# Window attention with sink keys and a gated MLP on one core: batch 1's q and k as four long-run loads, score tiles by keys, and a new order of all steps

## The chip, the core and the metric

The kernel runs on one core of a Trainium2 chip. A core has five engines that run their own instruction streams: PE (TensorE: matmuls and transposes into PSUM), DVE (VectorE), ACT (ScalarE), POOL (GpSimd) and SP (SyncE, here only an issuer of DMAs). They meet through semaphores. PSUM has eight banks of 128 x 512 float32. The metric is the device time of one execution in microseconds (us), measured over several runs.

## What is computed

Inputs are q, k, v of 4 batches, 8 heads, 768 positions and 64 features in float32. A position attends to the 128 positions up to and with itself, and to the first 4 positions ("sink" keys). The attention's output x (768 x 512 a batch) goes through a gated MLP with spatial mixing:

```python
scores = scale * np.matmul(q, k.transpose(0, 1, 3, 2))
keep = (pos[None, :] < n_sink) | ((rel >= 0) & (rel < window))     # n_sink 4, window 128
a = softmax(np.where(keep, scores, -1e9))
x = np.matmul(a, v)                         # to (batch, 768, 512)
h = gelu_tanh(x @ w_in)                     # 512 -> 1024
u, v = h[..., :512], h[..., 512:]
v_n = (v - mean) / sqrt(var + 1e-6) * g_ln  # over the 512 features
v_s = np.einsum('ts,bsd->btd', w_sg, v_n) + b_sg[None, :, None]   # w_sg 768 x 768
out = x + (u * v_s) @ w_out                 # 512 -> 512
```

## The kernel before

Matmuls are in bf16, their sums in float32. All work is cut into small steps. A string, STEPS, lists them in one order, and each step emits its instructions in that order on its engine; there is no scheduler. The framework adds the semaphore waits that the data need. A step's numbers are its batch and its tile; a last letter names the engine (A for ACT, D for DVE, P for POOL). The work of neighbouring batches is interleaved by hand in this list, so that PE has scores of one batch beside the MLP of another.

A batch goes through these steps. q, k and v are loaded. Batch 0's q and k come in float32 by head pair from SP (LPQ, LPK, L243), in runs of 1536 bytes, each partition holding six consecutive positions, and are cast to bf16 (CPQ, CPK). The others' q and k come through POOL's DMA queue, which converts to bf16 (LQ, LK, L223): six loads each of 128 positions x 8 heads, in rows of 256 bytes, 128 KB written a load. LVH (L269) loads v by four heads. q and k are then turned so that the features are on the partitions: TQ and TK on PE (batch 0 by head pair, L371; batches 1 and 2 by two tiles, L377) with EQ and EK to bring them to SBUF (L197 on ACT, L198 on DVE); batch 3 by DMA transposes on SP (DQ, DK). The constant HOW = "GBBC" chooses this by batch.

QK (L478) computes transposed scores of a head pair and a tile of 256 queries: 256 matmuls of 128 or 256 columns, in three pieces per tile (two for the first). EX (L483, ACT) takes the exponential, MK masks it (DVE L490, POOL L493 and L496; a few tiles get the mask as a bias matmul, L473). KS, SK (L457) and SX (L462) do the same for the sink keys. AV (L519, L523, L526) multiplies with v, with a 65th column of ones that sums the weights; NR (L535, L536, DVE) divides by that sum, 36 steps of one head pair and two or three tiles. x is turned by XT and XE (L545), or by DMA (XD) for later batches.

The MLP: MV (L561) multiplies x with the second half of w_in, GV (L565, ACT) is its gelu, BN (L574 to L578, DVE) its mean and variance, RS (L583) the power -1/2, on POOL, NM (L586) and Z (L592 on ACT, L595 on DVE) normalise. MU (L602) and GU (L607) do the first half, u. WT (L614) and WE turn w_sg once. SP (L622, a step on PE that has its name by chance in common with the engine SP) is the spatial mix, GT (L627, DVE) applies g_ln and b_sg, GM (L632, DVE or POOL) multiplies with u. OU (L639) is the last product, RA (L643, DVE) adds x, and ST stores 256 KB from SP.

The weights' loads are issued by POOL too: LW (L275, two halves of w_in), LWS (L280, two halves of w_sg), LWO (L283, w_out), LB (L299, b_sg to all partitions). So POOL has masks, products, the powers RS and the loads in one stream. Steps WARM, FILL, MASK, IDEN and HM (matmuls on zeros at the start, L188) prepare.

Buffers come from rings that are used round robin. PSUM has two double banks for wide tiles (sc) and four single banks (mm). A step that takes a buffer waits until the last reader of its old content is done:

```python
sc_ring = Ring("sc", 2, [128, 2, 512], F32, psum)
mm_ring = Ring("mm", 4, [128, 512], F32, psum)
q16 = Ring("q16", 2, [128, NT * d_model], BF16)
```

Of the kernel before, what the change touches and what calls it, by code (L numbers as in the profile page):

```python
# [14 lines left out]
HOW = "GBBC"  # L15
VHOW = "HHHH"
# [4 lines left out]
WARM LPQ.0 FILL LPK.0 LPK.1 LPQ.1 LPQ.2 LG MASK LPK.2 LPK.3 CPQ.0.A VSK LPQ.3 IDEN CPK.0.A IDEN2 MASK0 HM.9 TQ.0.0  # L21
TK.0.0 EQ.0.0.D EK.0.0.A VSO HM.3 QK.0.0.0 ZERO CPK.1.P QK.0.0.1.1 EX.0.0.0 LVH.0.0 EX.0.0.1 QK.0.0.2.1 CPQ.1.D TK.0.1
EX.0.0.2 LC CPQ.2.D LVH.0.1 TQ.0.1 MK.0.0.0.D EK.0.1.A TQ.0.2 EQ.0.1.D EQ.0.2.A HM.2 QK.0.1.0 CPK.2.A CPK.3.P
QK.0.1.1.1 EX.0.1.0 LQ.1.0 CPQ.3.D TK.0.2 EX.0.1.1 TK.0.3 EK.0.2.D LQ.1.1 TQ.0.3 EK.0.3.A GTR EQ.0.3.D LW.0 QK.0.2.0
QK.0.2.1 EX.0.2.0 LK.1.0 KS.0 VSM.0 HM.2 SK.0.2 EX.0.2.1 SK.0.1 MK.0.2.0.D HM.4 AV.0.0.0 LW.1 QK.0.3.0.1 MK.0.1.0.D
SX.0.1 SX.0.2 QK.0.3.1 MK.0.2.1.P GCP.D NR.0.0.0 EX.0.3.0 AV.0.0.1 AV.0.1.0 AV.0.1.1 NR.0.0.1 EX.0.3.1 QK.0.1.2
NR.0.1.0 AV.0.2.0 AV.0.3.0 EX.0.1.2 MK.0.3.1.P NR.0.1.1 QK.0.2.2 AV.0.2.1 NR.0.2.0 EX.0.2.2 TQ.1.0 NR.0.3.0 MK.0.1.2.P
QK.0.3.2 AV.0.3.1 EQ.1.0.A NR.0.2.1 XT.0.0 NR.0.3.1 LWS.0 AV.0.0.2 EX.0.3.2 AV.0.1.2 XE.0.0.D LK.1.1 XT.0.1 MK.0.2.2.D
# [47 lines left out]
def kernel(  # L76
# [29 lines left out]
    NH = S // 2  # L106

# [3 lines left out]

    class Ring:
        def __init__(self, name, n, shape, dtype, pool=sb):
            self.tiles = [pool.tile(shape, dtype, name=f"{name}{i}") for i in range(n)]
            self.used = 0
            self.held = {}

        def new(self, key):
            t = self.tiles[self.used % len(self.tiles)]
            self.used += 1  # L120
            self.held[key] = t
            return t
# [7 lines left out]
    sc_ring = Ring("sc", 2, [128, 2, 512], F32, psum)  # L130
    mm_ring = Ring("mm", 4, [128, 512], F32, psum)
    q16 = Ring("q16", 2, [128, NT * d_model], BF16)
    k16 = Ring("k16", 2, [128, NT * d_model], BF16)
    qT = Ring("qT", 2, [128, NT * d_model], BF16)
    kT = Ring("kT", 2, [128, NT * d_model], BF16)
    P = Ring("P", 10, [128, 2, 512], BF16)
    exs = Ring("exs", 2, [128, 512], BF16)
    x_sb = Ring("x_sb", 2, [128, NT, d_model], BF16)
    xT = Ring("xT", 2, [128, NT, KD, 128], BF16)
    z = Ring("z", 2, [128, NT, d_half], BF16)  # L140
    uT = Ring("uT", 2, [128, KU, S], BF16)
    vt = Ring("vt", 3, [128, 2, d_half], F32)
    gtmp = Ring("gtmp", 4, [128, NH], BF16)
    ot = Ring("ot", 6, [128, d_model], F32)
    mvs = Ring("mvs", 2, [128, NT, 2], F32)
    rs = Ring("rs", 2, [128, NT], F32)
    nmr = Ring("nmr", 2, [128, NT], F32)
    v_sb = Ring("v_sb", 2, [128, H, NT, Dh + 1], BF16)
    v_sink = Ring("v_sink", 2, [128, H, Dh + 1], BF16)
    ks_w = 128 // HP  # L150
    ks_sink = Ring("ks_sink", 2, [128, HP, ks_w], BF16)

    c16 = Ring("c16", 6, [128, d_model], BF16)
    iden = sb.tile([128, 128], BF16, name="iden")
# [22 lines left out]
    def gated(b, hf):  # L177
        return gatedT[:, slots.setdefault((b, hf), len(slots) % 3)]
# [532 lines left out]
```

## Time and profile before

| what | value |
|---|---|
| time, median of 3 runs | 156.51 us (156.33 to 158.79) |
| the profiled execution's own time | 157.69 us |
| its span, first to last instruction | 156.0 us, TensorE clock granted 1.000 |
| DVE / ACT / POOL, share of the span | 79% / 64% / 64% |
| SP's DMA queue (hardware): packets, MB | 21544, 13.41 |
| PE busy, 0 to 10 / 10 to 20 / 20 to 30 us | 8.55 / 8.69 / 9.56 us |
| PE busy, 30 to 50 / 50 to 60 / 60 to 70 us | 20.00 / 8.85 / 9.30 us |
| PE busy, 70 to 150 us | 79.95 of 80 us |

How to read it: the profile is of one execution, so sums over its rows are set against that execution's span, not against the median. A matmul's end is modelled in the records, and matmuls are pipelined, so PE's busy share is an upper bound of the time in which it is at its rate; starts of successive instructions tell the rate. The chain that ended last is followed back from the last instruction to what released each one. In the timelines a row holds the start (us), the duration, the engine, the line, the operation, output <- inputs, the tile's shape, how many instructions were put together, and in brackets the idle time before them with what ended it. For a DMA issue the duration is that of the instruction that issues it; the transfer itself lands later.

### The profile page before, as it was taken

To read this page: it belongs to the slowest core of one execution; us is meant where nothing else is said; L and a number is where in the kernel's file an instruction comes from. 1 tells how busy PE (TensorE), PEld (TensorE's weight loads), DVE (VectorE), ACT (ScalarE), POOL (GpSimd) and SP (SyncE) were. 2 spreads that over 40 slices of the span, in tenths; PEclk is the share of its full clock that TensorE was granted. 3 is DMA by queue.
4 is the path that set the end of the run, shared out by engine and by line. 5 is a ranking of instruction groups with operands and counts; after the bars stand their busy time and mean duration, and the time that the engine had idled before them with its cause. 6 is when DMAs were issued, how large, how long until landed. Compare 5 with 4: busy or idle time off the path is not lost.

```text
span 156.0 us, 3856 instructions
## 1 busy us (share of the span) xinstructions
PE 146.7 (94%) x1549; PEld 94.2 (60%) x1549; DVE 123.4 (79%) x295; ACT 99.0 (64%) x110; POOL 99.3 (64%) x127
## 2 busy tenths in 40 slices
PE   6988989999999979989999999999999999999990
PEld 2445577779675756747566764486567644776530
DVE  4557789829989969969789887899789956867981
ACT  3699798799899846276897855269954025591000
POOL 4099779388999899997549869640798610300400
PEclk9999999999999999999999999999999999999999
DMA  4999999999999999999999199995710580510064
GB/s 156 282 365 151 153 197 189 166 192 193 146 143 142 193 152 139 167 156 156 168 230 246 22 285 174 178 197 60 236 71 3 102 235 0 202 63 11 0 227 179
DMA packets 86170, 24.67 MB, mean 158 GB/s; under 512 B 78660, under 2 KB 83016, under 8 KB 86152
## 3 DMA queue, kind: packets, MB, share of 16 engines
q0 software_dynamic: 64608, 11.01, 94.9%
q1 hardware_dynamic: 21544, 13.41, 33.1%
q8 instruction: 12, 0.20, 0.5%
q14 instruction: 6, 0.05, 0.1%
HBM read 24.81 MB, written 6.29 MB: 199 GB/s over the span
## 4 chain that ended last, share of the span: by engine, by line
PE 73%; DMA 17%; DVE 2%; POOL 2%; issue 1%; ACT 1%; SPq 1%; ACTq 0%
PE mm L622 17%; PE mm L639 14%; PE sc L561 13%; PE sc L602 12%; DMA w_out_sb<-in_moe_w_out_dram 7%; DMA v_sb<-in_v_dram 6%; PE sc L478 4%; DMA uT<-in_k_dram 4%; PE mm L519 3%; PE mm L377 3%; PE mm L523 2%; PE mm L526 2%; PE mm L614 1%; POOL v_sb L269 1%; PE mm L545 1%
## 5 line engine op out<-in xcount | busy, mean ns | idle before, releaser
L483 ACT ACTIVATE P<-sc 128x1024 bf16<-128x1024 f32 (+1 forms) x48 | 43.4, 953 | 10.3 <-PE sc L478 10.1
L622 PE MATMUL mm<-wsgT,z 128*128 128x384 bf16 x192 | 34.1, 327 | 0.0
L622 PEld LDWEIGHTS <-z 128*128 128x128 bf16 x192 | 17.7, 98 | 11.9 <-issue 0.7
L639 PE MATMUL mm<-w_out_sb,wsg_gated 128*128 128x512 bf16 x96 | 22.7, 379 | 1.1 <-DMA w_out_sb<-in_moe_w_out_dram 1.1
L561 PE MATMUL sc<-w_in_sb,xT 128*128 128x512 bf16 x96 | 22.2, 379 | 0.7 <-ACT vt L565 0.7
L627 DVE SCALAR_TENSOR_TENSOR gtmp<-mm,g_sb,b_bc 128x384 bf16<-128x384 f32 x32 | 19.1, 611 | 4.2 <-PE mm L622 3.6
L602 PE MATMUL sc<-xT,w_in_sb 128*128 128x256 bf16 x192 | 22.1, 273 | 0.0
L493 POOL TENSOR_SCALAR_AFFINE_SELECT P<-P 128x512 bf16<-128x512 bf16 x21 | 14.0, 667 | 12.3 <-ACT P L483 12.0
L632 POOL TENSOR_TENSOR wsg_gated<-gtmp,uT 128x384 bf16<-128x384 bf16 x15 | 14.5, 982 | 10.9 <-DVE gtmp L627 10.9
L574 DVE BATCH_NORM_STATS2 st<-vt 128x6 f32<-128x512 f32 x24 | 15.4, 685 | 7.5 <-ACT vt L565 7.4
L602 PEld LDWEIGHTS <-w_in_sb 128*128 128x128 bf16 x192 | 18.7, 98 | 3.0
L536 DVE TENSOR_TENSOR x_sb<-mm,rcp 128x384 bf16<-128x384 f32 (+1 forms) x36 | 18.5, 513 | 1.2
L643 DVE TENSOR_TENSOR ot<-mm,x_sb 128x512 f32<-128x512 f32 x24 | 16.1, 684 | 2.7 <-PE mm L639 2.5
L565 ACT ACTIVATE vt<-sc 128x1024 f32<-128x1024 f32 x12 | 12.3, 1027 | 9.0 <-PE sc L561 8.9
L583 POOL TENSOR_TENSOR rs<-rs,neg_half 128x4 f32<-128x4 f32 (+1 forms) x8 | 6.9, 867 | 17.4 <-DVE rs L578 16.0
L223 POOL DMA_DIRECT2D k<-in_k_dram x18 | 16.4, 928 | 0.7 <-DMA v_sb<-in_v_dram 0.7
L223 POOL DMA_DIRECT2D q<-in_q_dram x18 | 16.7, 952 | 0.0
L519 PE MATMUL mm<-v_sb,P 128*128 128x65 bf16 x192 | 15.9, 194 | 0.7 <-DMA v_sb<-in_v_dram 0.6
L519 PEld LDWEIGHTS <-P 128*128 128x128 bf16 x192 | 14.5, 98 | 2.8 <-issue 0.6
L639 PEld LDWEIGHTS <-wsg_gated 128*128 128x128 bf16 x96 | 9.2, 98 | 11.4 <-DMA w_out_sb<-in_moe_w_out_dram 1.4
L561 PEld LDWEIGHTS <-xT 128*128 128x128 bf16 x96 | 9.2, 98 | 10.9 <-issue 0.9
L478 PE MATMUL sc<-qT,kT 64*128 64x128 bf16 (+1 forms) x256 | 14.8, 238 | 0.6 <-DVE qT L198 0.3
(90 smaller groups left out, 244.4 us busy)
## 6 DMA issues: line engine op xcount, KB each, us to landing
out_dram<-ot SPq DMA_DIRECT2D x24, 256.0 KB, 2.3
v_sb<-in_v_dram POOLq DMA_DIRECT2D x8, 384.0 KB, 8.3
q<-in_q_dram POOLq DMA_DIRECT2D x18, 128.0 KB, 6.7
k<-in_k_dram POOLq DMA_DIRECT2D x18, 128.0 KB, 6.9
wsg_gated<-in_moe_w_sg_dram POOLq DMA_DIRECT2D x2, 576.0 KB, 8.3
w_in_sb<-in_moe_w_in_dram POOLq DMA_DIRECT2D x2, 512.0 KB, 10.2
uT<-in_q_dram SPq DMA_DIRECT2D x2, 384.0 KB, 3.2
uT<-in_k_dram SPq DMA_DIRECT2D x2, 384.0 KB
```

The costliest lines, as they stand in the source:

```text
L223: return nc.gpsimd.dma_start(out=dst.rearrange("p (h d) -> p h d", h=H), in_=heads(src, b, i))
L478: nc.tensor.matmul(sc[:, hl, c:c + 128 * ni], at(kT, b)[rows, j, p, :], at(qT, b)[rows, i:i + ni, p, :], start=not biased, stop=(not biase ...
L483: nc.scalar.activation(out=P.new((b, p, g))[:, :, 0:w], in_=sc_ring[b, p, g][:, :, 0:w], func=AF.Exp, scale=scale)
L519: nc.tensor.matmul(av[:, il, hl, :], pt[:, hl, c:c + 128], vb[:, h, i, :], start=first, stop=False)
L536: nc.vector.tensor_mul(x_sb.get(b)[:, i0:i0 + n, 128 * p:128 * (p + 1)].rearrange("p t (h d) -> p t h d", h=2), av[:, :, :, 0:Dh], rcp[:, ...
L561: nc.tensor.matmul(hp[:, jl, :], xT[b][:, 2 * g + jl, c, :], w_in_sb[:, c, d_half:2 * d_half], start=(c == 0), stop=(c == KD - 1))
L574: nc.vector.bn_stats(out=sts[jl], in_=vt[b, g][:, jl, :])
L602: nc.tensor.matmul(hp[:, dc // 2, 256 * (dc % 2):256 * (dc % 2 + 1)], w_in_sb[:, c, 128 * dc:128 * (dc + 1)], xT[b][:, 2 * g:2 * g + 2, c, :],
L622: nc.tensor.matmul(ps[:, 0:NH], z[b][:, si, 128 * dc:128 * (dc + 1)], wsgT[:, si, NH * hf:NH * (hf + 1)], start=(si == 0), stop=(si == NT ...
L627: nc.vector.scalar_tensor_tensor(out=gtmp.new((b, hf, dc)), in0=mm_ring["g", b, hf, dc][:, 0:NH], scalar=g_sb[:, dc:dc + 1], in1=b_bc[:, N ...
L639: nc.tensor.matmul(ps, gated(b, hf)[:, dc, 128 * tl:128 * (tl + 1)], w_out_sb[:, dc, :], start=(dc == 0), stop=(dc == KU - 1))
L643: nc.vector.tensor_add(ot.new((b, t)), mm_ring["o", b, t], x_sb[b][:, t, :])
```

## The change

1. **Loads.** Batch 1's q and k are loaded with two loads each of four heads. A partition holds six consecutive positions, so a run is 6 x 64 float32 = 1536 bytes; 384 KB are written a load. They take the place of twelve tile loads. They are turned by head pair: 8 TQ and TK with 12 transposes each in the place of 6 with 8, and the copy to SBUF puts the positions in order again (a stride of six). Batches 2 and 3 keep tile loads.
2. **Score tiles by keys.** Tile g holds the products of keys of tiles 2g and 2g+1 with all the queries that need them. There are two pieces of up to 256 columns per tile (192 matmuls in all). Tile g = 2, not 0, is the one of 384 columns.
3. **AV and NR by four heads.** A step has a tile of two PSUM banks. There are 18 of each instead of 36.
4. **PSUM and rings.** All of PSUM is one tile of eight banks. Which buffer a step gets is written out in a table, SLOTS, for all rings. gtmp has 3 buffers, not 4; the two v tiles were used in turn by the batches (0, 1, 0, 1) and now go 0, 0, 1, 1. The last batch's output rows are held in the q16 and k16 tiles.
5. **Order.** STEPS is written anew for all engines. There are 12 warming matmuls instead of 20; SK and SX of batch 0 are one step each instead of two; Z has 13 steps on ACT and 11 on DVE (9 and 15 before), MK 27 on DVE and 17 on POOL (23 and 21), GM 18 on DVE and 14 on POOL (17 and 15).

The core of the diff (the long new list is cut to the stretch around the first spatial mix):

```diff
-HOW = "GBBC"
-VHOW = "HHHH"
+LAYOUT = "SGBM"
...
-MV.0.0 XE.0.1.A LK.1.2 NR.0.0.2 MK.0.3.2.D LK.1.3 NR.0.1.2 AV.0.2.2 AV.0.3.2 LQ.1.2 NR.0.2.2 GV.0.0 MV.0.1 NR.0.3.2
-LQ.1.3 BN.0.0 LWS.1 XT.0.2 GV.0.1 MU.0.1 XE.0.2.A BN.0.1 WT.0 GU.0.1 TK.1.0 MV.0.2 RS.0.1 EK.1.0.A LK.1.4 NM.0.1
-WE.0.A WT.1 GV.0.2 LK.1.5 TK.1.1 MU.0.2 LB.P EK.1.1.A BN.0.2 Z.0.0.A LK.2.0 WT.2 GU.0.2 MU.0.0 WE.1.D RS.0.2 WE.2.D
-Z.0.1.A LQ.2.0 NM.0.2 Z.0.2.A Z.0.3.D Z.0.4.D WT.3 LQ.2.1 WT.4 GU.0.0 WE.3.D WT.5 LQ.1.4 Z.0.5.D TQ.1.1 QK.1.0.0
-EQ.1.1.D QK.1.1.0 LQ.1.5 SP.0.0.0 WE.4.D LK.2.1 EX.1.0.0 VSM.1 SP.0.0.1 WE.5.D EX.1.1.0 LVH.1.0 GT.0.0.0 TK.1.2 KS.1
...
+LPK.3 TQ.0.1 EQ.0.1.D CPK.3.D CPQ.2.A TQ.0.2 LVH.0.0 EX.0.0.2 LVH.0.1 LQ.1.0 TK.0.2 LK.1.0 EX.0.0.1 EK.0.2.A LK.1.1
+GTR LW.0 QK.0.1.2 QK.0.1.0 LWS.1 EX.0.1.0 LPQ.3 LC EX.0.1.2 TK.0.3 EQ.0.2.D QK.0.2.0 EX.0.2.0 CPQ.3.D TQ.0.3 EQ.0.3.A
+LW.1 VSM.1 EK.0.3.D MK.0.2.0.D MK.0.1.0.D QK.0.1.1.1 EX.0.1.1 KS.0 GCP.D QK.0.3.2 EX.0.3.2 QK.0.3.0.1 VSM.0 LK.2.4
+MK.0.1.2.P LWS.0 SK.0 MK.0.3.2.D AV.0.0.0 NR.0.0.0 SX.0 QK.0.3.1 AV.0.0.1 NR.0.0.1 QK.0.2.1 EX.0.3.0 AV.0.0.2 EX.0.3.1
+EX.0.2.1 MK.0.2.1.P MK.0.3.1.D AV.0.1.0 NR.0.1.0 LQ.1.1 QK.0.2.2 EX.0.2.2 MK.0.2.2.P TQ.1.0 TQ.1.1 EQ.1.1.D EQ.1.0.A
+XT.0.0 XE.0.0.D LB.P TK.1.0 EK.1.0.A TK.1.1 NR.0.0.2 AV.0.1.1 NR.0.1.1 AV.0.1.2 NR.0.1.2 QK.1.0.0 LQ.2.2 LQ.2.4 LK.2.3
+EK.1.1.A QK.1.1.1 EX.1.1.1 TK.1.3 LK.2.2 LK.2.0 LQ.2.5 EK.1.3.D EX.1.0.0 TK.1.2 EK.1.2.A XT.0.2 XT.0.1 XE.0.1.D MV.0.0
+XE.0.2.D GV.0.0 BN.0.0 LK.2.5 LQ.2.0 MV.0.1 GV.0.1 MV.0.2 GV.0.2 BN.0.1 RS.0.1 WT.5 BN.0.2 WT.3 LK.2.1 NM.0.1 Z.0.0.D
+WE.3.A RS.0.2 WT.4 NM.0.2 Z.0.5.D Z.0.2.D MU.0.2 GU.0.2 LVH.1.1 Z.0.3.A WE.4.D MU.0.0 GU.0.0 Z.0.1.D WT.2 Z.0.4.A
+MU.0.1 GU.0.1 LQ.2.3 WE.5.D WT.1 WE.1.D LVH.1.0 MK.1.1.1.P TQ.1.2 EQ.1.2.A TQ.1.3 EQ.1.3.A SP.0.1.1 WT.0 WE.2.D
...
+SLOTS = """
+sc 040144164260240620461604044626041446404064620622066050602426460464604204204606462640466064
+mm 01223607302306723067626017010102326070123245452750102332676023232320275454320161402430430430
...
+v_sb 0011
...
-    sc_ring = Ring("sc", 2, [128, 2, 512], F32, psum)
-    mm_ring = Ring("mm", 4, [128, 512], F32, psum)
+    banks = psum.tile([128, 8, 512], F32, name="banks")
+    sc_ring = Ring("sc", [banks[:, i:i + 2, :] for i in range(7)])
+    mm_ring = Ring("mm", [banks[:, i, :] for i in range(8)])
...
+        if LAYOUT[b] == "G":
+            cols = slice(4 * NT * Dh * x, 4 * NT * Dh * (x + 1))
+            nc.gpsimd.dma_start(out=flat(ring, b)[:, cols].rearrange("p (h f) -> p h f", h=4),
+                                in_=src[b, 4 * x:4 * x + 4].rearrange("h (p t) d -> p h (t d)", p=128))
+            return
...
     def wide(g):
-        return 512 if g else 384
+        return 384 if g == NT // 2 - 1 else 512
...
-        pieces = [(2 * g, 2 * g, 2, 0), (2 * g + 1, 2 * g + 1, 1, 256)] + ([(2 * g - 1, 2 * g, 1, 384)] if g else [])
...
+        for n, (j, ni, c) in enumerate(((2 * g, 2, 0), (2 * g + 1, min(2, NT - 2 * g - 1), 256))):
...
-    def AV(b, p, k):
+    def AV(b, hq, k):
         vb = v_sb[b]
-        fresh(mm_ring, ("a", b, p, k))
-        av = av_view(b, p, k)
+        fresh(sc_ring, ("a", b, hq, k))
+        av = av_view(b, hq, k)
...
-    def RA(b, t):
-        nc.vector.tensor_add(ot.new((b, t)), mm_ring["o", b, t], x_sb[b][:, t, :])
+        row = last(b, t) if b == B - 1 else ot.new((b, t))[:, 0]
+        nc.vector.tensor_add(row, mm_ring["o", b, t], x_sb[b][:, t, :])
```

More of the change, by code (lines that the diff above doesn't have):

```diff
@@ L140, with ring @@
[L140 to L149, printed above, removed]
+    def ring(name, n, shape, dtype):
+        return Ring(name, [sb.tile(shape, dtype, name=f"{name}{i}") for i in range(n)])
@@ L161 @@
     headsel = sb.tile([128, H], F32, name="headsel")
+    quadsel = sb.tile([128, 4], F32, name="quadsel")
     halfsel = sb.tile([128, 2], F32, name="halfsel")
@@ L320, in FILL, with FILL2 @@
         nc.vector.memset(halfsel[64:128, 1:2], 1.0)
+    def FILL2():
+        nc.vector.memset(quadsel, 0.0)
+        for a in range(4):
+            nc.vector.memset(quadsel[32 * a:32 * a + 32, a:a + 1], 1.0)
+        for t in ks_quad.tiles:
+            nc.vector.memset(t, 0.0)
     def MASK():
@@ L476, in QK @@
             for hl in range(2):
                 rows = slice(64 * hl, 64 * hl + 64)
-                nc.tensor.matmul(sc[:, hl, c:c + 128 * ni], at(kT, b)[rows, j, p, :], at(qT, b)[rows, i:i + ni, p, :],
-                                 start=not biased, stop=(not biased or n == len(pieces) - 1))
+                nc.tensor.matmul(scs[0][:, hl, c:c + 128 * ni], at(kT, b)[rows, j, pq, :],
+                                 at(qT, b)[rows, j:j + ni, pq, :], start=not biased, stop=last)
     def EX(b, p, g):
@@ L518, in AV @@
                 c = 256 * (i % 2)
[L519 to L520 removed]
+                jobs.append((j // (2 * n), dst, P[b, p, i // 2][:, hl, c:c + 128], vb[:, head(b, hq, a), i, :]))
                 if i >= 1:
[L522 to L524 removed]
@@ new lines, in AV @@
+                    jobs.append((j // (2 * n), dst, P[b, p, (i - 1) // 2][:, hl, c:c + 128], vb[:, head(b, hq, a), i - 1, :]))
+                if i >= 2 and a % 2:
+                    h0, h1 = head(b, hq, a - 1), head(b, hq, a)
+                    jobs.append((j // (2 * n), av[:, j // (2 * n), j % (2 * n) - 1:j % (2 * n) + 1, :],
+                                 exs[b][:, 128 * (i - 2):128 * (i - 1)], v_sink[b][:, h0:h1 + 1:h1 - h0, :]))
+        for m, (bank, dst, lhsT, rhs) in enumerate(jobs):
+            nc.tensor.matmul(dst, lhsT, rhs, start=(m == 0 or jobs[m - 1][0] != bank),
+                             stop=(m + 1 == len(jobs) or jobs[m + 1][0] != bank))
```

428 lines of the change are left out of this document (227 added, 201 removed).

## The prediction

> **What bounds the kernel now.** I read the page first (busy shares, then the chain that ended last), then the timelines of PE and of POOL, then the times from issue to landing.
>
> ```profile
> span 156.0 us, 3856 instructions
> PE 146.7 (94%) x1549; PEld 94.2 (60%) x1549; DVE 123.4 (79%) x295; ACT 99.0 (64%) x110; POOL 99.3 (64%) x127
> ...
> q0 software_dynamic: 64608, 11.01, 94.9%
> ```
>
> PE is the busiest, but its 146.7 us counts pipelined matmuls to their modelled ends. The rate is read from the starts in PE's timeline:
>
> ```profile
> 1.25 4.02 PE L188 MATMUL mm<-warm 128*128 128x512 bf16 x9 [1.25 <-DVE warm L304]
> ...
> 29.22 1.91 PE L602 MATMUL sc<-xT,w_in_sb 128*128 128x256 bf16 x16
> 30.97 0.50 PE L614 MATMUL mm<-iden,wsg_gated 128*128 128x128 bf16 x6
> ...
> 40.07 2.12 PE L622 MATMUL mm<-wsgT,z 128*128 128x384 bf16 x12
> 42.03 0.61 PE L377 MATMUL mm<-iden,k 128*128 128x128 bf16 x8
> ...
> 56.35 1.04 PE L639 MATMUL mm<-w_out_sb,wsg_gated 128*128 128x512 bf16 x4 [1.15 <-DMA w_out_sb<-in_moe_w_out_dram]
> ```
>
> The reader is to subtract starts: an MU takes 30.97-29.22 = 1.75 us, two SPs 42.03-40.07 = 1.96. In the same way an MV is 1.73, an OU 0.865, a TQ or TK 0.447 (by tile) or 0.38 (by head pair), a WT 0.335, an XT 0.447, an SK 0.33, a warming matmul 0.216, a QK 0.275 (0.22 where 384 wide; 0.54 more where biased), an AV of three rows 0.365 or 0.535 (of batch 0: 0.19 or 0.357). By these PE has 140.5 us of work. Its last matmul ends at 151.9, so 11.4 us are lost. The first SP marks the place best: it starts at 40.07 with 32.9 us of work behind it. So 7.2 us are lost before it and 4.2 after; of the 4.2, 1.15 is the wait for w_out_sb above. What ends last before the first SP is the chain MV, GV, BN, RS, NM, Z. RS is a power that runs on POOL, and POOL also issues the loads, in the order of the steps:
>
> ```profile
> 27.93 0.78 POOL L280 DMA_DIRECT2D wsg_gated<-in_moe_w_sg_dram  x1
> 31.83 1.04 POOL L583 TENSOR_TENSOR rs<-rs,neg_half 128x4 f32<-128x4 f32 x1 [3.12 <-DVE rs L578]
> 32.84 1.86 POOL L223 DMA_DIRECT2D k<-in_k_dram  x2
> ...
> 41.85 2.87 POOL L269 DMA_DIRECT2D v_sb<-in_v_dram  x2
> ...
> 52.40 1.82 POOL L223 DMA_DIRECT2D k<-in_k_dram  x2 [0.72 <-DMA v_sb<-in_v_dram]
> ```
>
> Two things are to be seen. At 31.83 RS finds POOL idle. At 52.40 a load's *issue* stood 0.72 us because an older load had not landed: it is LK.2.4, the eighth load after LVH.1.1, which was issued at 43.3 and took 8.6 to 9. The order of instructions as built has the same wait on every POOL load from the ninth on: it is issued only when the eighth before it has landed. Whatever stands behind it on POOL waits too.
>
> **The change, part by part.**
>
> *PE's work* falls to 138.4 us: 8 warming matmuls fewer (8 x 0.216 = -1.73), one SK fewer (-0.33), scores in two pieces instead of three (the fit 0.22 = 384 columns and 2 pieces, 0.275 = 512 and 3, gives 0.265 and 0.215: -0.40), and batch 1's turning, 8 x 0.38 = 3.04 for 6 x 0.447 = 2.68 (+0.36). The sum is -2.1.
>
> *DVE*: 18 merged normalisations (12 of 768 elements, 6 of 512) for 36. Rows: 384 elements 0.558, 256 elements 0.425, so 1.04 ns an element: 0.96 and 0.69, and about 0.19 for the reciprocal: 12 x 1.15 + 6 x 0.87 = 19.0 us for 23.4 (from the rows' spacing, 24 x 0.70 + 12 x 0.55). Masks on DVE are 27 for 23 (about 0.65 each, +2.6), casts and copies shift between ACT and DVE; DVE's total stays near 123 us. It saves nothing on the path. In the opening it even has 20.4 us of steps before MV.0.0 instead of 14.4 (batch 1's turned tiles, and all of NR.0 before XT): from about 7 us on without a gap that is 27.5, and MV.0.0 comes no earlier than 28.5 instead of 24.6.
>
> *Transfers.* Twelve loads of batch 1 (1024 rows of 256 bytes read, 128 KB written) become four of 512 runs of 1536 bytes (384 KB written). No row shows a converting load of such runs. Nearest rows, from issues and landings: LVH, the same bytes in 3072 rows, lands 2.85 us after its predecessor (17.7, 20.5); the halves of w_in, 512 KB in 512 rows, 2.55 and 2.6; the plain pair loads of 384 KB written in 1536-byte runs come 1.05 apart (7.84, 8.89, 9.9). So one costs from 1.05 to 2.85. I take 1.95, w_in's rate by bytes, since that row is a converting load of long runs. The others: halves of w_sg 2.7 and 2.75, a small load 0.45 to 0.85 (0.65), b_bc 0.9 (39.8 after 38.9).
>
> The v halves of batch 0 keep their place behind CPK.1.P, so the second lands at 20.5 as before. Then, in the new order of issue: LQ.1.0 22.45, LK.1.0 24.4, LK.1.1 26.35, LW.0 28.9, LWS.1 31.65, LW.1 34.25, LK.2.4 34.9, LWS.0 37.6, LQ.1.1 39.55, LB 40.45.
>
> **The step that decides.** In the new order eight loads stand ahead of RS.0.1 on POOL without other work between them: LQ.2.2, LQ.2.4, LK.2.3, LK.2.2, LK.2.0, LQ.2.5, LK.2.5, LQ.2.0. The last waits for the eighth before it, LB. So POOL stands until 40.45; LQ.2.0's issue 0.93 (row of L223), RS.0.1 1.04, then LK.2.1 0.93 (the load it waits for, LQ.2.2, lands right behind LB), RS.0.2 0.71: 44.05. Behind RS wait, on DVE, NM.0.2 0.15 and Z.0.5, Z.0.2, WE.4, Z.0.1, WE.5, WE.1, 0.55 each: 47.5. On ACT, Z.0.3 stands ahead of GU.0.0, whose bank WT.1 needs. The first SP (SP.0.1.1) needs all Z and WE.3 to WE.5, and WE.1's bank: 47.6 instead of 40.07. PE itself would be there at 41.8: MV.0.0 from 28.9, when w_in has landed, and 12.9 of work (3 MV, 3 MU, 5 WT, 2 TQ). So the order costs 5.8 us, at the ends of a load's price 2.2 and 9.4.
>
> *From there* 106.8 us of PE work remain (138.4-31.6). Losses after it: I count 0.5 at AV.1.1.0 (a mask late on DVE), 0.9 at AV.3.0.0 (batches 2 and 3 now share one v tile, so LVH.3.0 is issued only after AV.2.1.1; at 6.9 to 10.1 to landing it is 0 to 1.7 late), 0.4 at SP.3 (two GUs behind GM.2.1.1): 1.8. The wait for w_out_sb goes, since PE comes to it some 10 us later than before. Bounds for the sum are 0 and the 4.2 of before. The masks, copies and stores are hidden behind this PE work; if their cover failed, it is DVE that is late next, with 123 us in all.
>
> *The clock.* PE stands about 3.6 us before WT.1 and again before TQ.1.3. After the 1.15 us gap at 56.35 the matmuls run at the usual 0.216, so that gap cost nothing; the first nine of the run took 4.02 us instead of 1.94, so a cold start costs 2.1. This stall lies between the rows: 0 to 2.1, and I take 1.0, the middle, since neither row is nearer.
>
> The Trainium skill (TensorE: Matmul & The Clock Gate, Part 1: The HAM clock gate) says that PE falls to half its clock after about one idle window of 3.4 us and needs about as long to come back. The first nine matmuls agree with it; no row has a stall of this length in mid-run. By it the term would be up to 1.7 instead of 1.0, which would put the time 0.7 higher.
>
> The span: 47.6 + 106.8 + 1.8 + 1.0 + 4.1 (last matmul to the end, 156.0-151.9) = **161.3**. The profiled execution took 157.69 around a span of 156.0; the median of the three runs, 156.51, is 0.5 above the span. I give the median: **161.8 us**, 3.4% slower. About 2% (3.1 us) is what a measurement of this kernel tells from no change.
>
> **The rivals.**
>
> *The loads are faster than I price them* (1.05 us each): LB lands at 36.9, the first SP starts at 44.0, and with no clock term: 44.0+106.8+1.8+4.1+0.5 = 157.2. For it: runs six times as long. Against it: w_in's long rows. The Trainium skill (DMA: Bandwidth & Descriptors, Anatomy of one DMA) fits a POOL load as a fixed 2 us of latency and its bytes over 436 GB/s. If written bytes counted, that would be an estimate of 0.9 us and the time about 156.6; by the bytes read it is 1.8. The w_in rows agree with the bytes read.
>
> *POOL does not hold RS* (the wait for the eighth load is not what ended 52.40). Then the first SP is PE's, 41.8, and the median is 155.0: no difference.
>
> *Faster*: the same, and the wide score tiles and free banks take all later losses: 41.8+106.8+4.1+0.5 = 153.2, 2.1% faster. It decides in the first SP: it must start by 42. Against it stand the eight issues in a row.
>
> *Slower still*: loads at 2.85 put the first SP at 51.2, with 4.2 of later losses and the full clock term: 51.2+106.8+4.2+2.1+4.1+0.5 = 168.9.
>
> **How the numbers follow.** Forecast 0.57 (158 to 165), faster loads 0.16, RS not held 0.09, faster 0.12, slower still 0.06. Leaving out the fastest case and the far end of the slowest gives 154.5 to 166.5. Slower by over 2% (above 159.6) is the slowest case and 0.54 of the forecast: 0.60; faster 0.12; the same, the rest, 0.28.
>
> **What would show it.** In the profile of the changed kernel: POOL's row of RS.0.1 starts at 41 to 43 directly behind a chain of load issues with idle time that a DMA ends; ACT and DVE wait for RS; the first L649 matmul starts at 46 to 49; PE's starts from there to its end span 108 to 111 us. Wrong would be: RS.0.1 before 38, a first SP before 44, or over 5 us lost after it.

## The result, and the profile after

The changed kernel takes **170.73 us** (median of 4 runs, 169.27 to 171.11) against 156.59 for the kernel before: 1.0865 times as long, with a 95% interval from 1.0793 to 1.0936. Ratios, here and below, are the recorded estimates over the fast runs alone and times are medians of all runs, so a ratio is not the quotient of two times shown (here 1.090). The forecast was slower, at 161.8, with a range up to 166.5. The direction was right, and the time lies above the range. The profiled execution took 169.27 us, with a span of 167.6.

The page of the changed kernel (the row PEclk is the granted clock of PE in 40 slices of 4.2 us, in tenths):

```profile
span 167.6 us, 3772 instructions
...
PE 148.3 (89%) x1521; PEld 93.8 (56%) x1521; DVE 127.8 (76%) x262; ACT 99.8 (60%) x112; POOL 85.6 (51%) x111
...
PEclk9999999999759999999999999999999999999999
...
q0 software_dynamic: 54240, 11.01, 80.6%
```

The long runs took a sixth of the packets off POOL's queue (64608 before), the bytes are the same. PE's busy share fell from 94% to 89%, and near 46 us the clock falls to half; in the kernel before every slice of that row is a 9.

The place that the prediction looked at is POOL's stream ahead of RS.0.1 (L609; loads are L254). The bracket is the idle time before a row and what ended it:

```profile
28.26 0.88 POOL L254 DMA_DIRECT2D q<-in_q_dram  x1 [0.54 <-DMA w_in_sb<-in_moe_w_in_dram]
30.89 0.88 POOL L254 DMA_DIRECT2D k<-in_k_dram  x1 [1.75 <-DMA wsg_gated<-in_moe_w_sg_dram]
33.88 1.76 POOL L254 DMA_DIRECT2D k<-in_k_dram  x2 [2.11 <-DMA w_in_sb<-in_moe_w_in_dram]
37.05 0.88 POOL L254 DMA_DIRECT2D q<-in_q_dram  x1 [1.40 <-DMA wsg_gated<-in_moe_w_sg_dram]
39.03 0.88 POOL L254 DMA_DIRECT2D k<-in_k_dram  x1 [1.11 <-DMA q<-in_q_dram]
40.02 0.88 POOL L254 DMA_DIRECT2D q<-in_q_dram  x1
40.91 1.06 POOL L609 TENSOR_TENSOR rs<-rs,neg_half 128x4 f32<-128x4 f32 x1
41.92 0.94 POOL L254 DMA_DIRECT2D k<-in_k_dram  x1
42.89 0.77 POOL L609 TENSOR_TENSOR rs<-rs,neg_half 128x2 f32<-128x2 f32 x1
```

Five times POOL stands at a load's issue until another load has landed, and each time the one it waits for is the eighth before it (LW.0, LWS.1, LW.1, LWS.0, LQ.1.1). RS.0.1, whose input DVE had ready at 35.8, starts at 40.91 right behind. Of these 5.1 us about 2.3 are waits for landings, and 2.6 are the issues of LQ.2.5, LK.2.5 and LQ.2.0 themselves, 0.88 each. What PE does meanwhile, up to the first spatial mix (L648):

```profile
39.30 1.91 PE L628 MATMUL banks<-xT,w_in_sb 128*128 128x256 bf16 x16
44.02 0.68 PE L640 MATMUL banks<-iden,wsg_gated 128*128 128x128 bf16 x6 [2.82 <-ACT uT L633]
...
48.13 0.85 PE L399 MATMUL banks<-iden,q 128*64 128x128 bf16 x12 [2.64 <-DVE wsgT L225]
48.91 2.10 PE L648 MATMUL banks<-wsgT,z 128*128 128x384 bf16 x6
```

PE stands twice, 2.8 and 2.6 us, at WT.1 and at TQ.1.3. The first mix takes 1.9 us from its start to the next step (50.81) instead of 0.98: it runs at half clock.

Between the powers and TQ.1.3 stands DVE, and it is slower there than usual. Its rows of Z (L621):

```profile
43.89 2.32 DVE L621 TENSOR_SCALAR z<-vt,rs,nmr 128x512 bf16<-128x512 f32 x2
...
46.59 1.02 DVE L621 TENSOR_SCALAR z<-vt,rs,nmr 128x512 bf16<-128x512 f32 x1
```

Three Z take 3.3 us here, while the seven later ones on DVE take 0.54 to 0.61 each. Why these are slow was not tested.

Further on, DVE waits for stores, which the prediction had called hidden. RA (L686) writes a result into an `ot` buffer, and its rows show what held the buffer:

```profile
74.05 0.69 DVE L686 TENSOR_TENSOR ot<-banks,x_sb 128x512 f32<-128x512 f32 x1 [0.18 <-PE banks L681]
...
81.28 0.69 DVE L686 TENSOR_TENSOR ot<-banks,x_sb 128x512 f32<-128x512 f32 x1 [2.06 <-DMA out_dram<-ot]
...
114.17 0.69 DVE L686 TENSOR_TENSOR ot<-banks,x_sb 128x512 f32<-128x512 f32 x1 [1.78 <-DMA out_dram<-ot]
```

The row at 74.05 is RA.0.0, the row at 81.28 is RA.0.1. By the written list "011021..." both use buffer 1, though buffers 2 to 5 are free. RA.0.0's store went out at 74.77 and landed at 81.25, 6.5 us later, against a median of 2.3. POOL's loads and the two transposes of x that SP had issued just before were under way at the same time; c4 below bears on that. DVE's late additions then hold PSUM banks that PE needs:

```profile
84.24 0.41 PE L550 MATMUL banks<-v_sb,P 128*128 128x65 bf16 x8 [0.80 <-DVE ot L686]
...
108.98 1.89 PE L587 MATMUL banks<-w_in_sb,xT 128*128 128x512 bf16 x8 [1.11 <-DVE ot L686]
...
114.91 1.02 PE L681 MATMUL banks<-w_out_sb,wsg_gated 128*128 128x512 bf16 x4 [1.05 <-DVE ot L686]
```

The first row lies inside AV.2.0.0 and the last is OU.1.4; both wait for an RA that stands behind one held by a store, or is itself held. The middle one is MV.2.1 (the expectations below call it the wait of MV.2.0): its bank is freed by RA.1.5, which no store held.

**Where the 11.6 us of span come from.** From the start of each PE step to the next I subtracted the usual spacing of its kind (an SP 0.98, an MV 1.73, and so on). The first mix starts 8.8 us later than before (48.91 for 40.07). From there to the last matmul's end it is 114.3 us for 111.8. Of the 114.3, some 105.4 are work and 8.9 are lost: 1.1 at half clock, 2.2 by the stores (1.0 in AV.2.0.0, 1.2 at OU.1.4), 1.3 at MV.2.1 (the RA.1.5 that frees its bank stands behind three masks on DVE) and 4.3 in pieces of about 0.5 and less. The medians differ by more than the spans, 14.1 us; the reason is given further on.

### The profile page after: what moved, and what is told of

The parts are those of the page before. It is cut to its first block, busy times and chain, and to the rows that moved or that the text cites. A ratio compares the mean times of both kernels' runs of the same rounds, so it can differ in the third digit from the quotient of the medians.

```text
span 167.6 us, 3772 instructions
## 1 busy us (share of the span) xinstructions
PE 148.3 (89%) x1521; PEld 93.8 (56%) x1521; DVE 127.8 (76%) x262; ACT 99.8 (60%) x112; POOL 85.6 (51%) x111
## 4 chain that ended last, share of the span: by engine, by line
PE 44%; DMA 27%; DVE 13%; ACT 4%; POOL 4%; issue 3%; SPq 2%; DVEq 0%; ACTq 0%
PE banks L648 16%; DMA q<-in_q_dram 11%; PE banks L681 10%; DMA out_dram<-ot 7%; PE banks L628 6%; DMA z<-in_k_dram 5%; DMA w_out_sb<-in_moe_w_out_dram 4%; PE banks L587 4%; PE banks L550 3%; DVE ot L686 3%; PE banks L495 3%; ACT P L500 2%; ACT z L618 2%; DVE P L507 2%; DVE st L600 1%
## 5 line engine op out<-in xcount | busy, mean ns | idle before, releaser
L500 ACT ACTIVATE P<-banks 128x1024 bf16<-128x1024 f32 (+1 forms) x48 | 42.9, 954 | 8.3 <-PE banks L495 7.9
L648 PE MATMUL banks<-wsgT,z 128*128 128x384 bf16 x192 | 35.1, 332 | 0.3 <-ACT uT L633 0.3
L669 DVE SCALAR_TENSOR_TENSOR gtmp<-banks,g_sb,b_bc 128x384 bf16<-128x384 f32 x32 | 19.2, 611 | 11.2 <-PE banks L648 9.4
L648 PEld LDWEIGHTS <-z 128*128 128x128 bf16 x192 | 18.3, 99 | 13.4 <-issue 2.3
L681 PE MATMUL banks<-w_out_sb,wsg_gated 128*128 128x512 bf16 x96 | 23.2, 379 | 1.1 <-DVE ot L686 1.1
L587 PE MATMUL banks<-w_in_sb,xT 128*128 128x512 bf16 x96 | 22.2, 379 | 1.5 <-DVE ot L686 1.1
L628 PE MATMUL banks<-xT,w_in_sb 128*128 128x256 bf16 x192 | 22.1, 273 | 0.0
L507 DVE TENSOR_TENSOR P<-P,mask 128x1024 bf16<-128x1024 bf16 (+1 forms) x27 | 18.6, 708 | 1.0 <-ACT P L500 1.0
L550 PE MATMUL banks<-v_sb,P 128*128 128x65 bf16 x352 | 16.2, 194 | 0.8 <-DVE ot L686 0.8
L587 PEld LDWEIGHTS <-xT 128*128 128x128 bf16 x96 | 9.3, 98 | 12.8 <-issue 1.4
L564 DVE TENSOR_TENSOR x_sb<-banks,rcp 128x768 bf16<-128x768 f32 (+1 forms) x18 | 15.6, 869 | 0.6
L686 DVE TENSOR_TENSOR ot<-banks,x_sb 128x512 f32<-128x512 f32 x18 | 12.2, 684 | 5.0 <-DMA out_dram<-ot 4.6
L495 PE MATMUL banks<-qT,kT 64*128 64x256 bf16 x192 | 14.4, 262 | 1.5 <-ACT P L500 0.5
```

Of the source, the lines that this page charges most:

```text
L495: nc.tensor.matmul(scs[0][:, hl, c:c + 128 * ni], at(kT, b)[rows, j, pq, :], at(qT, b)[rows, j:j + ni, pq, :], start=not biased, stop=last)
L500: nc.scalar.activation(out=P.new((b, p, g))[:, :, 0:w], in_=sc_ring[b, p, g][:, :, 0:w], func=AF.Exp, scale=scale)
L507: nc.vector.tensor_mul(pt[:, :, 0:w], pt[:, :, 0:w], m.unsqueeze(1).to_broadcast([128, 2, w]))
L550: nc.tensor.matmul(dst, lhsT, rhs, start=(m == 0 or jobs[m - 1][0] != bank), stop=(m + 1 == len(jobs) or jobs[m + 1][0] != bank))
L564: nc.vector.tensor_mul(rows, av[:, :, :, 0:Dh], rcp.to_broadcast([128, 2, 2 * n, Dh]))
L587: nc.tensor.matmul(hp[:, jl, :], xT[b][:, 2 * g + jl, c, :], w_in_sb[:, c, d_half:2 * d_half], start=(c == 0), stop=(c == KD - 1))
```

## The experiments

Step names are those of the order list. All runs were compared with the kernel before on their own chip. The chips differ by up to 0.6%, so ratios stand beside the times. The first mix and the end of the last matmul are from each run's profiled execution. Score tiles by keys, the merged AV and NR, and the PSUM table (parts 2 to 4 of the change) were not run alone.

| run | what is changed | us | ratio to before (95%) | first mix | last matmul ends |
|---|---|---|---|---|---|
| before | | 156.6 | | 40.07 | 151.8 |
| changed | | 170.73 | 1.0865 (1.079 to 1.094) | 48.91 | 163.2 |
| a1 | 2 loads behind the powers | 166.99 | 1.063 (1.057 to 1.069) | 45.96 | 161.7 |
| a2 | 9 loads behind the powers | 169.84 | 1.080 (1.074 to 1.086) | 42.09 | 163.2 |
| a3 | six output buffers | 167.05 | 1.060 (1.054 to 1.067) | 48.48 | 160.7 |
| a4 | PE kept busy in its stalls | 167.35 | 1.065 (1.061 to 1.069) | 48.78 | 162.0 |
| b1 | before, with the long loads | 161.12 | 1.025 (1.018 to 1.031) | 41.54 | 155.3 |
| c2 | 4 loads behind, six buffers | 159.97 | 1.017 (1.009 to 1.024) | 42.17 | 154.0 |
| c3 | c2, other loads moved | 167.80 | 1.063 (1.052 to 1.075) | 42.05 | 162.5 |
| c4 | c2, x of batch 1 turned on PE | 161.96 | 1.029 (1.022 to 1.036) | 41.46 | 155.6 |
| d1 | 4 loads behind, nothing else | 162.06 | 1.037 (1.033 to 1.040) | 41.65 | 155.8 |
| d2 | powers of batch 0 left out | 162.75 | 1.040 (1.036 to 1.043) | 42.20 | 156.8 |
| d3 | a2, six buffers | 168.48 | 1.078 (1.074 to 1.081) | 41.38 | 160.8 |
| d4 | c2, three masks later | 160.26 | 1.024 (1.022 to 1.026) | 41.30 | 154.2 |

### a1: two of the eight loads behind the powers

```diff
-... GV.0.0 BN.0.0 LK.2.5 LQ.2.0 MV.0.1 ... RS.0.2 WT.4 ...
+... GV.0.0 BN.0.0 MV.0.1 ... RS.0.2 LK.2.5 LQ.2.0 WT.4 ...
```

> The changed kernel, with only the last two of the eight loads (LK.2.5, LQ.2.0) behind RS.0.2 instead of ahead of RS.0.1. Theory 'held powers' (POOL stands until the eighth load before has landed): RS.0.1 then follows LQ.2.5, whose issue ended at 37.93, so it starts at about 38 instead of 40.9; RS.0.2 about 3 us earlier, the first spatial mix at about 46 instead of 48.9, and the time falls by 2.9 to 3.5 us, to about 167.5. Rival 'issue time' (the powers are late because POOL is busy issuing, 0.9 us a load): 1.8 us earlier and 169. Rival 'late data' (the long loads make w_in, w_sg and x late, and the powers' place doesn't matter): below 0.5 us.

POOL in this run:

```profile
37.89 0.87 POOL L254 DMA_DIRECT2D q<-in_q_dram  x1 [1.38 <-DMA wsg_gated<-in_moe_w_sg_dram]
38.78 1.06 POOL L609 TENSOR_TENSOR rs<-rs,neg_half 128x4 f32<-128x4 f32 x1
```

RS.0.1 starts 2.1 us earlier and not 2.9, because LQ.2.5 itself was issued later in this run (37.89 for 37.05). From that issue to the power it is 0.89 us, where it was 3.86: 1.8 of the 3.0 are the two issues and 1.1 is the wait for a landing. So "issue time" (1.8) is not the whole cause, and the powers stood behind both. The first mix comes at 45.96, 2.95 us earlier, in part because the clock falls only at 46.84. The median falls by 3.7, the profiled execution by 1.1: in it, 1.4 more was lost behind the first mix. "Late data" gave under 0.5 and is out.

### d1 and d2: the four loads alone, and no power at all

```diff
-... LK.2.2 LK.2.0 LQ.2.5 ... BN.0.0 LK.2.5 LQ.2.0 ... RS.0.1 ... LK.2.1 ... RS.0.2 ...
+... LK.2.2 LK.2.0 ... BN.0.0 ... RS.0.1 ... RS.0.2 LQ.2.5 LK.2.5 LQ.2.0 LK.2.1 ...
```

> The changed kernel with the four loads alone (LQ.2.5, LK.2.5, LQ.2.0, LK.2.1) behind RS.0.2, buffers as they were: the run at 159.97 without its six output buffers. If the two faults add up, the buffers are worth what they were in the changed kernel (3.7 us): 163.5. If they overlap (the stores are late only because everything is), the time is near 160.

```diff
     def RS(b, g):
         r = rs[b][:, part(g)]
-        nc.gpsimd.tensor_tensor(r, r, neg_half[:, part(g)], op=ALU.pow)
+        if b:
+            nc.gpsimd.tensor_tensor(r, r, neg_half[:, part(g)], op=ALU.pow)
```

> The changed kernel with batch 0's two powers (RS.0.1, RS.0.2) left out, so batch 0 is scaled by its variance and not by its root's inverse; no load is moved. What waits for POOL then waits for nothing there. Theory 'held powers': NM.0.1 runs at about 36 instead of 42, the first spatial mix starts at 41.5 to 42.5, the clock stays up, and the time is within 1 us of the run with four loads moved (163.5). Rival: moving the loads itself made the gain (other transfers come sooner), so that without a move less than half of the 7 us appears: 167 or more.

d1 takes 162.06 us and d2 162.75. In d2 no load was moved, and DVE goes on at once (L613 is NM):

```profile
37.27 0.15 DVE L613 SCALAR_TENSOR_TENSOR nmr<-mvs,rs 128x4 f32<-128x4 f32 x1
```

In the changed kernel it ran at 42.00. Two edits with nothing in common but that the chain no longer waits for POOL give the first mix at 41.65 and 42.20, and 8.7 and 8.0 us less, what the half clock cost included (it stays up in both). This is the larger of the two faults, and it is shown. The first mix at 41.65 to 42.2 also bears out the 41.8 that the prediction gave for PE alone.

### a3: six output buffers

```diff
-ot 011021022020111200
+ot 012345012345012345
```

> The changed kernel, with the output buffers ot used round robin, all six, instead of the written list that uses three. Theory 'store buffers': the three waits of RA for a store (4.6 us of DVE) go, and with them the PE stalls that DVE's RA ended (at 83.0, 106 to 109 and 112.8 to 114.9: 0.96+1.27+1.21 = 3.4 us); the time falls by 2.5 to 3.5 us, to about 167.7. Rival: what the stores hold up is late anyway (exponentials, masks) and the time stays within 1 us.

3.7 us less (2.4 between the profiled executions). From the first mix to the last matmul it is 112.3 us for 114.3, and the stalls in AV.2.0.0 and at OU.1.4 are gone. The 1.3 at MV.2.1 stays, so that part of the expectation was wrong: it is DVE's own order, not a store. Beside the four moved loads the same edit is worth 2.1 by the times (162.06 in d1, 159.97 in c2) and 3.2 by the ratios, against 4.1 by the ratios here: whether the faults overlap is not clear of the noise.

### a4: what the half clock costs

```diff
-... Z.0.4.A MU.0.1 GU.0.1 ... MK.1.1.1.P TQ.1.2 EQ.1.2.A ...
+... Z.0.4.A HM.13 MU.0.1 GU.0.1 ... MK.1.1.1.P HM.12 TQ.1.2 EQ.1.2.A ...
```

> The changed kernel, with 13 matmuls on zeros put ahead of MU.0.1 and 12 ahead of TQ.1.2, where PE stands for 2.8 and 2.6 us in the changed kernel; they add 5.4 us of PE work inside these stalls. If the stalls cost nothing but their own length, the time stays (or grows by up to 0.5 us). If the fall of the granted clock to half (44.2 to 51.0 us) costs what the rows say (0.7 us before the first spatial mix, 1.1 behind), the clock stays at 1.00 and the time falls by 1.1 to 1.8 us.

```profile
38.77 2.97 PE L215 MATMUL banks<-warm 128*128 128x512 bf16 x12
...
44.55 2.75 PE L215 MATMUL banks<-warm 128*128 128x512 bf16 x12
...
48.31 0.53 PE L399 MATMUL banks<-iden,q 128*64 128x128 bf16 x12 [0.56 <-DVE wsgT L225]
48.78 1.14 PE L648 MATMUL banks<-wsgT,z 128*128 128x384 bf16 x6
```

5.4 us of useless matmuls make the kernel faster. The granted clock is 1.00 up to the last matmul, and the first mix takes 0.98 us. It starts nearly where it did (48.78): TQ.1.3 takes 0.47 us for 0.78, but DVE frees its bank 0.2 later in this run. The profiled execution gains 1.4 us (167.88 for 169.27), as expected, the median 3.4. The changed kernel's four executions lie between 169.27 and 171.11 and its profiled one is the fastest; in a4 they lie between 166.89 and 167.88. So the half clock costs 1.4 us between the two executions whose traces are there. What more the others lost, and whether to the clock, is not shown; their mean granted clocks, 0.970 to 0.975, are little below the 0.978 of the profiled one.

### a2 and d3: why moving nine loads gives nearly nothing

```diff
-... QK.1.0.0 LQ.2.2 LQ.2.4 LK.2.3 EK.1.1.A ... LK.2.2 LK.2.0 LQ.2.5 ... LK.2.5 LQ.2.0 ... LK.2.1 ... RS.0.2 ...
+... QK.1.0.0 EK.1.1.A ... RS.0.2 LQ.2.2 LQ.2.4 LK.2.3 LK.2.2 LK.2.0 LQ.2.5 LK.2.5 LQ.2.0 LK.2.1 ...
```

> The changed kernel, with all eight loads and LK.2.1 moved behind RS.0.2; nothing else is moved. Theory 'held powers': RS.0.1 starts when its input is there, 35.8; the first spatial mix is then PE's, at 42 to 43 instead of 48.9; PE no longer stands long enough for the clock to fall (1.8 us were lost at half clock between 44.2 and 51.0), so the time falls by 7 to 8 us, to about 163. Rival 'late data': the moved loads land late instead, batch 2's turning waits for them, and most of the gain is lost again: 168 or more.

The first mix is at 42.09, as foretold, and the time only 0.9 us lower, which the two intervals do not tell from nothing. The rival's 168 or more is what came, and this was the largest miss of the study. d3 takes the store buffers out of the comparison.

> All nine loads behind RS.0.2 (the run at 169.84) with six output buffers. Against the run at 159.97 only five loads (LQ.2.2, LQ.2.4, LK.2.3, LK.2.2, LK.2.0) stand elsewhere: ahead of the powers there, from 26.7 to 35.6, behind them here, from 38.0 on. If late loads are what gave the gain back, 165.5 to 167 (169.84 less 3 to 4 for the buffers); if it was the store buffers in another place, 160 to 161.

d3 takes 168.48, c2 159.97: 8.5 us for the place of five loads. (d3 lies above the 165.5 to 167 expected.) The columns of the next rows are the stretch, its length, the busy time of PE, PEld, DVE, ACT and POOL, the clock, the DMA share (the time of all packets over the time of 16 engines, above 1 where packets overlap), and GB/s. First c2, where the five are issued from 26.7 on, then d3, where they follow the powers:

```profile
36.00:40.00 4.00, 4.00 (x42) 3.62 (x41) 3.73 (x10) 2.94 (x5) 3.44 (x5) 1.00 1.72 231
```

```profile
36.00:40.00 4.00, 4.00 (x42) 3.63 (x40) 3.72 (x11) 3.45 (x4) 3.43 (x6) 1.00 0.91 159
```

In d3 POOL issues no load between 26.0 and 37.3, and the DMA share in this stretch is about half, 0.91 for 1.72. PE's waits in d3 show where it is paid, mostly at MV.1.1 (L587), for batch 1's x turned by DMA:

```profile
PE banks L587 <- DMA xT<-x_sb: 3.9, 1, 3.9
```

The wait is 1.1 in c2. The second transpose of x lands 9.5 us after its issue here, 6.6 after in c2, and the clock stands at half for 3.41 us behind the stall (76.88 to 80.29). That late loads give the gain back is shown by the pair. That they do it by colliding with the transposes of x is only argued: no run turned d3's x on PE.

### c2, c3, c4: the two cures together, and two edits that did not help

c2 is d1's order with a3's buffers.

> The changed kernel with only those loads moved behind RS.0.2 that would hold the powers (LQ.2.5, LK.2.5, LQ.2.0, LK.2.1), and with six output buffers. The first spatial mix is at 42 as in the run with all nine loads moved. That run lost 4.2 us at MV.1.1 (waiting for x turned by DMA), 1.35 at OU.0.3 (w_out), 1.8 at TK.2.0 and TQ.2.1 (batch 2's loads). Theory 'loads collide' (with the powers early, what ends last is POOL's loads, which share the DMA engines with XD.1 and the stores): the five loads ahead go out 2 to 6 us earlier, so TK.2.0 and TQ.2.1 no longer wait, but MV.1.1 and w_out still do; with the buffers' 3.4 us the time is about 164 to 165. Rival 'only the powers and the buffers': 170.7 - 7 - 3.5 = 160.

159.97: the rival's 160, not my 164 to 165. I had taken a2's later waits for a bound that would stay; they belonged to a2's late loads. Here MV.1.1 waits 1.1 us for x and w_out is on time.

```diff
-... GU.0.2 LVH.1.1 ... LVH.2.1 LK.3.0 ... GT.0.1.3 LQ.3.2 ... NR.1.1.1 LWO ... LK.3.5 ... LK.3.2 GV.1.1 ... GU.1.2 LK.3.1 ...
+... GU.0.2 LWO LVH.1.1 ... LVH.2.1 ... GT.0.1.3 ... NR.1.1.1 ... GV.1.1 ... GU.1.2 LK.3.0 LQ.3.2 LK.3.2 LK.3.5 LK.3.1 ...
```

> As the run before it, and POOL's loads set apart from XD.1: w_out's load goes out ahead of batch 1's v, and four of batch 3's loads (LK.3.0, LQ.3.2, LK.3.2, LK.3.5) go behind batch 2's second v load. Theory 'loads collide': XD.1 lands in 4 to 7 us instead of 10, the wait at MV.1.1 falls below 1.5 us and that for w_out goes: 3 to 5 us less than the run before it, about 160.5. Rival: XD.1 is slow whatever runs beside it, and the time changes by less than 1 us.

```profile
PE banks L495 <- DMA qT<-q: 4.0, 1, 4.0
...
PE banks L405 <- DMA q<-in_q_dram: 1.5, 1, 1.5
```

7.3 us worse by the ratios, not 4 better. Batch 2's q is late for TQ.2.1 (1.5 us), and batch 3's transposes, whose loads went out later, are late for the scores (4.0 us). That the first comes from w_out's earlier place is only likely, since the run makes both moves at once.

```diff
-... AV.1.0.1 XD.1.0 SK.2 ... NR.1.0.1 XD.1.1 QK.2.0.0 OU.0.3 ...
+... AV.1.0.1 XT.1.0 XE.1.0.D SK.2 ... NR.1.0.1 QK.2.0.0 XT.1.1 XE.1.1.A XT.1.2 XE.1.2.D OU.0.3 ...
```

> As the run with six buffers and four loads moved, but batch 1's x is turned on PE (XT, XE; 3 x 0.447 us of PE, 0.7 to 1.0 us each on DVE or ACT) instead of by DMA; the loads stay where they are. Theory 'loads collide': the wait at MV.1.1 goes (about 4 us) for 1.3 us of PE work, so the time is 2 to 3 us less, about 162; w_out is still waited for (1.2 us). Rival: PE waits as long for something else there (masks, exponentials) and the time grows by the 1.3.

2.0 us slower: the wait at MV.1.1 was 1.1 here, not 4, and the turning on PE costs 1.3 and a wait for x_sb of 1.3. It shows one thing of use: without batch 1's two transposes on SP, no store whose landing the trace gives took over 3.7 us (6.9 in c2).

### d4: three masks later

```diff
-... GM.1.0.3.D MK.3.1.0.D QK.3.2.1 MK.3.3.0.D ... OU.1.3 MK.3.1.1.D ... RA.1.3 RA.1.5 MV.2.0 ...
+... GM.1.0.3.D QK.3.2.1 ... OU.1.3 ... RA.1.3 RA.1.5 MK.3.1.0.D MK.3.3.0.D MK.3.1.1.D MV.2.0 ...
```

> The run at 159.97 with three masks of batch 3 (MK.3.1.0, MK.3.3.0, MK.3.1.1; 2.77 us of DVE) behind RA.1.3 and RA.1.5 instead of ahead of them. The wait of MV.2.0 (1.1 us, a bank that RA frees) goes: 1.0 to 1.3 us less, about 158.8. Rival: the masks are then late for AV.3.0.0, and the time stays.

```profile
97.47 3.62 PE L587 MATMUL banks<-w_in_sb,xT 128*128 128x512 bf16 x16
...
101.81 1.02 PE L681 MATMUL banks<-w_out_sb,wsg_gated 128*128 128x512 bf16 x4 [0.72 <-ACT vt L591]
...
105.95 1.02 PE L681 MATMUL banks<-w_out_sb,wsg_gated 128*128 128x512 bf16 x4 [0.82 <-DVE ot L686]
```

MV.2.0 and MV.2.1 now run without a gap, and the time does not fall (160.26; 159.97 in c2, on another chip, with overlapping intervals of the ratios). The wait has moved to the OU steps behind, at 0.7 and 0.8 us: for GV's bank and again for RA.

### b1: the long loads alone, in the kernel before

```diff
-HOW = "GBBC"
+HOW = "GGBC"
-... LQ.1.0 ... LQ.1.1 ... LW.0 ... LK.1.0 ... LK.1.1 ... LK.1.2 ... LQ.1.2 ... TQ.1.1 QK.1.0.0 ... VSM.1 ... TK.1.2 KS.1 ... TQ.1.2 ...
+... LQ.1.0 ... LW.0 ... LK.1.0 ... LK.1.1 ... LQ.1.1 ... TQ.1.1 QK.1.0.0 ... VSM.1 TK.1.2 WE.5.D TQ.1.2 ... TK.1.3 TQ.1.3 EK.1.3.A EQ.1.3.D KS.1 ...
```

> The kernel before, with the first part of the change alone: batch 1's q and k as four loads of four heads, turned by head pair (8 turnings instead of 6). The changed kernel's POOL rows give such a load 1.95 to 2.0 us of the queue (38.98 after 37.0), three times a tile load's 0.65, so four take as long as the twelve they replace; POOL has 8 us fewer of issues, PE 0.4 us more. Theory 'order': the long loads are not what made the changed kernel slow, and the time stays within 1.5 us of before. Rival 'long loads': they push w_in and w_sg back by up to 2 us each and the batch's turning costs more, so a good part of the 14 us shows here: 3 us or more.

3.6 us more, 2.5%: my "within 1.5" was wrong, and the rival's 3 us or more came. PE's waits in this run:

```profile
PE sc L478 <- DVE qT L198: 1.9, 3, 0.8
...
PE mm L614 <- DMA wsg_gated<-in_moe_w_sg_dram: 0.9, 1, 0.9
```

The first mix is 1.5 us later than before, and the other 1.9 at the last matmul come behind it. Scores wait for the copies that put the turned positions in order, w_sg lands later, and batch 1 has two turnings more to be done before its scores. It is one placement; a better one may exist.

No run beats the kernel before. The best of the changed ones, c2, is still 1.7% slower (0.9 to 2.4). Of its 2.1 us more at the last matmul all stand before the first mix (42.17 for 40.07); b1 points at the long loads and the turning, but which of them it is was not separated.

## Why the prediction was wrong

**Right: the step that decides.** RS.0.1 was put behind LQ.2.0's issue, at about 41.4, and started at 40.91; the first mix was put at 47.6 and came at 48.91. PE stood where it was said to, before WT.1 (2.8 us for 3.6) and TQ.1.3 (2.6). The 1.3 us too few are mostly DVE's: Z was put at 0.55, and the three Z behind RS.0.2 took 3.3 us for 1.65. TQ.1.3 at half clock added 0.4, and the powers were done 0.4 early. The landings that carried it came 0.4 to 0.8 earlier than forecast: LW.0 28.3 (28.9), LWS.1 30.9 (31.65), LW.1 33.9 (34.25), LWS.0 37.0 (37.6), LQ.1.1 39.0 (39.55). The long load's price, 1.95 chosen between 1.05 and 2.85, is 39.0 - 37.0 = 2.0. (LB, which the sum had last, held nothing: LQ.2.0's issue at 40.02 waited for no landing.) The rival "POOL does not hold RS" fell in a1, d1 and d2, "the loads are faster" by the price. "Slower still" named 168.9 and came nearest to the time, but by another mechanism (loads at 2.85), so that is luck. "Faster" needed a first mix by 42.

**Wrong: the losses behind the first mix.** "The masks, copies and stores are hidden behind this PE work" is the step that failed. I counted 1.8 us, at AV.1.1.0, AV.3.0.0 and SP.3, and bounded the sum by the 4.2 of before. None of the three places lost over 0.2. What came was 7.8, the half clock's 1.1 not counted: 2.2 by the stores (a3 took 2.0 off), which the lists of buffers could have told, since the same `ot` buffer is taken twice in a row; 1.3 by DVE's masks at MV.2.1 (d4 removed that wait); 4.3 in small pieces whose causes were not sought. "Over 5 us lost after it" was one of the prediction's own signs of being wrong. My bound was the old order's loss, and nothing in it bounds a new order.

**Mis-sized: the clock, the work and the median.** The clock term was 1.0 between 0 and 2.1. By the rows it is 1.5 in the profiled execution (0.4 at TQ.1.3, 1.1 behind the first mix's start), and a4 puts it at 1.4. From the Trainium skill (TensorE: Matmul & The Clock Gate, Part 1: The HAM clock gate) the prediction had estimated up to 1.7. The size is near, but the trace does not follow that working: the clock fell after a stall of 2.8 us, shorter than the idle window of 3.4 us that the Trainium skill names there, and stayed at half for 6.83 us, 2.6 of which PE stood.

The work left from the first mix was put at 106.8 and is some 105.4. A score step in two pieces takes about 0.22 us (0.17 where 384 wide), not the 0.265 and 0.215 of the fit. So the losses were missed by more than the sum shows.

The step from span to median, 0.5, was taken from the kernel before. There and here an execution takes 1.7 us more than its span (157.69 and 156.0; 169.27 and 167.6). But the profiled execution of the kernel before was 1.2 slower than the median, which hid most of that step, and the changed kernel's was the fastest of four, 1.5 below the median: 170.73 - 167.6 = 3.1.

**The sum.** 161.8 forecast; 1.3 at the first mix, 4.7 between it and the last matmul (114.3 for 109.6, the clock's 1.0 included: 6.0 more lost, 0.1 more at half clock, 1.4 less work), 0.3 in the tail and 2.6 from span to median give 170.7.

## What to carry to other kernels

In this kernel as built, a load's issue on POOL is a wait as soon as eight loads are under way (five times in the rows above), so a short instruction on the path (here a power of 1 us) must not stand behind a run of them; look where the eighth load before lands. Move only those loads that would hold it: moving five more cost as much as the cure had gained. A list of buffers written by hand is to be read like the order: each reuse is a wait for the last reader, a store among them, and a store is slow (6.5 us for 2.3) just when loads and transposes run.

## What the runs showed of the hardware

The granted clock falls and comes back in steps of one length: it is 0.5 for 6.83 us in the changed kernel (44.19 to 51.02) and in a3, and for 3.41 us in a1, a2, d3 and twice in c3. Within each trace all its changes lie a whole number of 3.41 us apart (in the changed kernel 6.64, 44.19, 51.02 and 167.07: 11, 2 and 34 steps). The Trainium skill (TensorE: Matmul & The Clock Gate, Part 1: The HAM clock gate) gives a free-running window of 3.4 us, and the lengths agree. The Trainium skill says there that the clock falls after an idle window, and here less is enough. In a1 PE stood 2.1 us of the 3.41 before the clock fell (46.84), and in c3 1.5 us before it fell at 53.80. The rows of c3 (L405 is TQ.2.1, L648 the mix behind it, usually 1.14):

```profile
51.93 0.39 PE L405 MATMUL banks<-iden,q 128*128 128x128 bf16 x4
53.78 0.61 PE L405 MATMUL banks<-iden,q 128*128 128x128 bf16 x4 [1.46 <-DMA q<-in_q_dram]
55.50 1.98 PE L648 MATMUL banks<-wsgT,z 128*128 128x384 bf16 x6
```

The length of the stall alone does not decide. In d2 PE stood as long, within one such step (104.99 to 108.40, counted from the clock's rise at 6.00), and the clock stayed up:

```profile
108.21 1.02 PE L682 MATMUL banks<-w_out_sb,wsg_gated 128*128 128x512 bf16 x4 [1.53 <-DVE ot L687]
```

What else it takes is open. Waits of 1.1 to 1.2 us (w_out in the kernel before, x in c2) left the clock up too. A stall of PE of 1.5 us can thus cost more than its own length, and need not.
